# A fused attention and mixing kernel: the third batch's strided products later, their copies spread inside them, and the last sums tile by tile

## Chip, cores and metric

The kernel runs on one core of a Trainium2 chip. The metric is the device time of one execution in microseconds (us). Before the change it is 918.03 us, the median of three runs (916.94 to 919.47).

## Reference

Eight batches of 576 rows go through attention with eight heads of 64. Heads 0 to 3 see a local window of 32 rows, heads 4 to 7 see the earlier rows that lie a multiple of 32 away. The result `x` (576 x 512 per batch) goes through a mixer along the rows and a two-layer network.

```python
rel = pos[:, None] - pos[None, :]
mask_local = (rel >= 0) & (rel < stride)
mask_strided = (rel >= 0) & (pos[None, :] % stride == pos[:, None] % stride)
masks = np.stack([mask_local if h < H // 2 else mask_strided for h in range(H)], axis=0)
scores = np.where(masks[None, :, :, :], scores, -1000000000.0)
...
attn = attn / (np.sum(attn, axis=-1, keepdims=True) + 1e-09)
return np.matmul(attn, v).astype(np.float32)

xt = x.transpose(0, 2, 1)
h = xt @ U @ V
u = x + h.transpose(0, 2, 1)
ch = np.maximum(u @ w_ch1, 0.0) @ w_ch2
return (u + ch).astype(np.float32)
```

`U` is 576 x 32, `V` is 32 x 576, `w_ch1` is 512 x 2048 and `w_ch2` 2048 x 512.

## The kernel before

**Stages.** The network runs over nine stages n = 0 to 8. Stages 0 to 7 hold the first 512 rows of a batch, stage 8 the last 64 rows of all eight batches together. A stage has 16 steps `fc`, one for each 128 columns of the hidden layer. A step has twelve matmuls of 128 x 512 into `ph` (`gemm1`, L668), the ReLU on ScalarE (`gh`, L673), a correction on VectorE (`gl`, L674), and twelve matmuls into four sums `acc` (`gemm2`, L686). The matmuls are in threes, because each factor is split in a high and a low part: `gh` and `gl` of the hidden layer, `uh` and `ul` of `u`, parts 0 and 1 of a weight. `gemm2` of a step comes one step late, behind `gemm1` of the next. At a stage's end `finish(n)` (L693) adds the four sums to `xg` on VectorE and issues the output.

**The next batch meanwhile.** While stage n runs, the attention of batch n + 1 is made. The local heads use TensorE (`px`). For batches 2 to 7 the strided heads are vector work with all 18 rows of a class in one partition (`strided_heads`). GpSimd multiplies queries and keys (`tmp<-st`, L467) and VectorE reduces to scores `s_st` (L445). After the softmax the values are loaded into the place of the keys (`st`). GpSimd multiplies weights and values (`tmp<-st,s_st`, L495), and VectorE reduces again, to `st<-tmp` (L445). Row i needs i + 1 products of 64 elements; from row 9 on they are cut into two halves of 32 columns. Five `tmp` buffers lie between the two engines. ScalarE then copies the rows into `xg` and the tail `xt` (L512, L516). The mixing step follows: `mix_t` (L536), `mix_u` (L558), `mix_tail` (L567), the transposes to `bt` on VectorE (L638), and 32 transfers `raw<-bt` on SyncE's queue (L96). From `raw` ScalarE and VectorE make `uh` (L659) and `ul` (L660), which the next stage's `gemm1` reads.

**Order.** Every engine and queue works in its own order of instructions. A scheduler in the compiler sets it from the order of the program and its own estimate of times. In the program, `advance(slot)` is called twice per step, with slots 32 per stage. It takes from the generators as many pieces of work as `A_EARLY`, `A_LATE` and `A_TAIL` (first slot, last slot, count) and `S0` and `S1` (first and last slot of the strided work) ask for. `strided_end` draws what is left of the strided work before the copies. A reduce of the strided work is held behind the latest `finish` that the program has emitted (`reduced`, with `marks["out"]`).

**Start.** Stage 0 also converts the weights, which arrive as 64-bit numbers (`cv`, L131 and L132; `w`, L206), beside the strided scores of the third batch, b = 2.

Of the kernel before, what the change touches and what calls it, by code (L numbers as in the profile page):

```python
# [16 lines left out]
ATT_BUFS = 5  # L17
NSP = 2
N_EARLY = 17
N_LATE = 47  # L20
N_STRIDED = 66
LAG = 1
CLA = 4
N_FIRST = 6
N_LEAD = 4
BEHIND = 5
A_EARLY = (5, 28, N_EARLY)
A_LATE = (2, 26, N_LATE)
A_TAIL = (4, 20, 8)
S0 = {2: 16, **{b: 32 * (b - 1) - 12 for b in range(3, 8)}}  # L30
S1 = (12, 12)
ORDER0 = (2, 3, 0, 1)
WARM = {0: 8, 1: 8}
PAIR = 2 * 576 + 18 * 65
# [3 lines left out]
def fused_kernel(ctx, tc, pairs, strided, U, V, w_in, masks, eye, out):  # L38
# [53 lines left out]
    def psx1():  # L92
        return psx2()[:, 0, :]
# [121 lines left out]
            next(wl["gen"])  # L215
            wl["n"] += 1

    xgs, tails, tsts, o_str = {}, {}, {}, {}
    halves = [slice(64 * hh, 64 * hh + 64) for hh in range(2)]

    def load_qk(b, pr):
# [225 lines left out]
    def strided_heads(b):  # L447

        st = wide_buffer("st")
        sq, sk = (st[:, x * NCH * D:(x + 1) * NCH * D].rearrange("p (i d) -> p i d", d=D) for x in range(2))  # L450
        if b == NSP:
            nc.gpsimd.tensor_copy(out=st[0:1, 0:1], in_=word_of[units.index((10, None))])
        dma(out=st, in_=strided[b - NSP, :, 0:2 * NCH * D])
        yield
        s_st = att([128, NCH, NCH], "s_st")
        nc.gpsimd.memset(s_st, 8.0 * NEG)
        late = []

        def flush(n):
            while len(late) > n:  # L460
                late.pop(0)()

        for i in range(NCH):
            for j0 in range(0, i + 1, 9):
                n = min(9, i + 1 - j0)
                tmp = att([128, 9, D], "tmp")
                nc.gpsimd.tensor_tensor(out=tmp[:, 0:n], in0=sk[:, j0:j0 + n], in1=sq[:, i:i + 1].broadcast_to([128, n, D]),  # L467
                                        op=ALU.mult)
                late.append(lambda tmp=tmp, n=n, i=i, j0=j0: reduced(
                    out=s_st[:, i, j0:j0 + n], in_=tmp[:, 0:n], axis=AX.X, op=ALU.add))  # L470
# [12 lines left out]
        nc.vector.tensor_reduce(out=m_st, in_=s_st, axis=AX.X, op=ALU.add)  # L483
        nc.vector.tensor_scalar(out=m_st, in0=m_st, scalar1=1e-9, scalar2=None, op0=ALU.add)
        nc.vector.reciprocal(out=m_st, in_=m_st)
        nc.vector.tensor_tensor(out=s_st, in0=s_st, in1=m_st.broadcast_to([128, NCH, NCH]), op=ALU.mult)
        yield
        o_st = sq
        o_str[b] = o_st
        for i in range(NCH):  # L490
            step = D if i < 9 else D // 2
            for d0 in range(0, D, step):
                tmp = att([128, (i + 1) * step], "tmp")
                tv = tmp.rearrange("p (j d) -> p j d", d=step)
                nc.gpsimd.tensor_tensor(out=tv, in0=sv[:, 0:i + 1, d0:d0 + step],  # L495
                                        in1=s_st[:, i, 0:i + 1].broadcast_to([128, i + 1, step]), op=ALU.mult)
                late.append(lambda tv=tv, i=i, d0=d0, step=step: reduced(
                    out=o_st[:, i, d0:d0 + step], in_=tv.rearrange("p j d -> p d j"), axis=AX.X, op=ALU.add))
                flush(1)
                yield  # L500
        flush(0)
        yield

    def strided_copies(b):
        xg, xt = x_tiles(b)
        tb = 64 * (b % 2)
        o_st = o_str[b]
        for h in range(4):
            rows = slice(32 * h, 32 * h + 32)
            cs = slice(256 + D * h, 256 + D * h + D)  # L510
            for i4 in range(4):
                nc.scalar.copy(out=xg[32 * i4:32 * i4 + 32, :, cs], in_=o_st[rows, i4:16:4, :])  # L512
                if i4 % 2:
                    yield
            for i4 in range(2):
                nc.scalar.copy(out=xt[tb + 32 * i4:tb + 32 * i4 + 32, cs], in_=o_st[rows, 16 + i4, :])  # L516
            yield

    ud = dp.tile([B // 2, 128, DM], F32, name="ud", bufs=1)

# [95 lines left out]
    def attention(b):  # L616
        if b >= NSP:
            yield from local_pairs(b)
            yield "strided"
            yield from strided_copies(b)  # L620
            yield from mix_t(b)
            yield
            yield from mix_u(b)
            yield from mix_tail(b)
            yield from transposes(b)
        else:
            yield from mix_tail(0)
# [47 lines left out]
        marks.setdefault("gl", []).append(low.ins)  # L675
        return gh, gl

    def gemm2(n, fc, gh, gl):
        if fc == 0:
            accs[n] = [ps_acc.tile([128, 2, 512], F32, name="acc") for _ in range(2)]  # L680
        for s in range(4):
            cs = slice(128 * s, 128 * s + 128)
            if fc == 0 and n == 0:
                nc.tensor.matmul(accs[n][s // 2][:, s % 2, :], Vst[:, cs], tsts[n], start=True, stop=False)
            for i, (gt, part) in enumerate(((gh, 0), (gh, 1), (gl, 0))):
                last = nc.tensor.matmul(accs[n][s // 2][:, s % 2, :], gt[:, cs], w_parts[fc, 1][:, part, :],  # L686
                                        start=(fc == 0 and i == 0 and n > 0), stop=(fc == NFC - 1 and i == 2))
        marks.setdefault("acc", []).append(last.ins)

    def finish(n):  # L690
        for s in range(4):
            ot = xgs[n][:, s, :]
            last = nc.vector.tensor_tensor(out=ot, in0=accs[n][s // 2][:, s % 2, :], in1=ot, op=ALU.add)  # L693
# [158 lines left out]
```

## Time and profile before

| | |
|---|---|
| median of three runs | 918.03 us |
| profiled execution | 918.08 us |
| its span | 916.0 us |
| granted TensorE clock, mean | 0.993 |
| ScalarE busy | 253.2 us (28%) |
| VectorE busy | 548.3 us (60%) |
| GpSimd busy | 339.4 us (37%) |

The profile was taken in one execution. A row of its timeline gives the start in us from the start of the span, the duration, the engine, the source line, the operation and `out<-in` with the shapes, and how many such instructions ran one after another. In brackets stands how long the engine was idle before the row, and what released it. `SPq` and `ACTq` are the DMA issues of SyncE and ScalarE. A row of the groups gives a line's count, busy time, mean duration in ns, and idle time before it. A row of the waits gives who waited for what, the total, the number, and the longest.

The chain that ended last runs through `acc` and `ph`:

```profile
PE acc L686 40%; PE ph L668 39%; PE px L397 1%; DMA w<-in_w_dram 1%; PE px L357 1%; PE px L379 1%; DVE s_st L445 1%; PE px L536 1%; PE px L558 1%; DVE cv L132 1%; DMA st<-in_strided_dram 1%; DVE w L206 1%; DMA od<-x 1%; DVE gl L674 0%; POOL tmp L467 0%
```

### The profile page before, as it was taken

How to read it: one execution, taken by the hardware profiler on the slowest of the kernel's cores; microseconds unless marked ns; L12 is line 12 of the kernel's file. 1: busy time of each engine (PE TensorE's matmuls, PEld its weight loads, DVE VectorE, ACT ScalarE, POOL GpSimd, SP SyncE). 2: the span in 40 equal slices, each digit the busy share in tenths (PEclk: the TensorE clock that was granted, in tenths of full speed). 3: DMA queues.
4: the chain of work that ended last, by engine and by line, in shares of the span. 5: the costliest groups of instructions: out<-in, count | busy, mean ns of one | idle time of the engine just before them, and what ended most of it. 6: DMA issues, size and time to landing. Idle time of an engine off the chain costs nothing.

```text
span 916.0 us, 16587 instructions
## 1 busy us (share of the span) xinstructions
PE 893.4 (98%) x6862; PEld 714.1 (78%) x6862; DVE 548.3 (60%) x899; ACT 253.2 (28%) x501; POOL 339.4 (37%) x378
## 2 busy tenths in 40 slices
PE   7899989999999999999999999999999999999997
PEld 4677768887888787878887888878787888888885
DVE  4678997856786588738873877477754331122111
ACT  3456422241224122521242123312241211121110
POOL 1232484636563475429450946175620000000000
PEclk9899999999999999999999999999999999999999
DMA  9869313210331015011401050103200230001001
GB/s 355 308 211 357 118 44 116 72 53 3 86 135 42 12 52 183 1 53 31 165 28 53 21 187 28 53 9 124 91 1 3 57 116 23 1 1 47 0 1 47
DMA packets 30843, 75.27 MB, mean 82 GB/s; under 512 B 6464, under 2 KB 14672, under 8 KB 28848
## 3 DMA queue, kind: packets, MB, share of 16 engines
q1 hardware_dynamic: 29360, 71.07, 22.6%
q0 software_dynamic: 1088, 2.62, 0.9%
q8 instruction: 54, 0.88, 0.4%
q10 hardware_dynamic: 320, 0.52, 0.2%
q14 instruction: 21, 0.17, 0.1%
HBM read 54.14 MB, written 11.67 MB: 72 GB/s over the span
## 4 chain that ended last, share of the span: by engine, by line
PE 84%; DVE 4%; DMA 2%; POOL 1%; issue 1%; ACT 1%; SPq 0%; DVEq 0%; POOLq 0%; ACTq 0%
PE acc L686 40%; PE ph L668 39%; PE px L397 1%; DMA w<-in_w_dram 1%; PE px L357 1%; PE px L379 1%; DVE s_st L445 1%; PE px L536 1%; PE px L558 1%; DVE cv L132 1%; DMA st<-in_strided_dram 1%; DVE w L206 1%; DMA od<-x 1%; DVE gl L674 0%; POOL tmp L467 0%
## 5 line engine op out<-in xcount | busy, mean ns | idle before, releaser
L674 DVE SCALAR_TENSOR_TENSOR gl<-ph,gh 128x512 fp32r<-128x512 f32 x144 | 98.5, 685 | 233.7 <-ACT gh L673 232.9
L467 POOL TENSOR_TENSOR tmp<-st 128x576 f32<-128x576 f32 (+6 forms) x162 | 177.0, 1128 | 127.6 <-DMA st<-in_strided_dram 71.7
L668 PE MATMUL ph<-uh,w 128*128 128x512 f32 x648 | 215.4, 391 | 0.0
L673 ACT ACTIVATE gh<-ph 128x512 fp32r<-128x512 f32 x144 | 85.7, 597 | 449.0 <-PE ph L668 424.8
L686 PE MATMUL acc<-w,gh 128*128 128x512 f32 x648 | 196.3, 391 | 0.0
L495 POOL TENSOR_TENSOR tmp<-st,s_st 128x448 f32<-128x448 f32 (+7 forms) x162 | 137.0, 876 | 128.2 <-DVE st L445 51.2
L686 PEld LDWEIGHTS acc<-w,gh 128*128 128x128 f32 x648 | 121.2, 188 | 26.8 <-issue 1.2
L668 PEld LDWEIGHTS ph<-uh,w 128*128 128x128 f32 x648 | 121.7, 188 | 26.0
L445 DVE TENSOR_REDUCE st<-tmp 128x64 f32<-128x64 f32 (+8 forms) x162 | 135.6, 882 | 2.6 <-POOL tmp L495 2.1
L668 PE MATMUL ph<-ul,w 128*128 128x512 f32 x324 | 126.4, 390 | 0.0
L686 PE MATMUL acc<-w,gl 128*128 128x512 f32 x324 | 121.8, 391 | 4.2 <-DVE gl L674 4.2
L445 DVE TENSOR_REDUCE s_st<-tmp 128x9 f32<-128x576 f32 (+6 forms) x162 | 86.4, 561 | 14.0 <-POOL tmp L467 13.4
L686 PEld LDWEIGHTS acc<-w,gl 128*128 128x128 f32 x324 | 60.8, 188 | 18.7 <-DVE gl L674 5.9
L668 PEld LDWEIGHTS ph<-ul,w 128*128 128x128 f32 x324 | 60.8, 188 | 12.5
L512 ACT COPY xg<-st 32x256 f32<-32x256 f32 x96 | 38.8, 404 | 10.7 <-DVE st L445 9.0
L660 DVE TENSOR_TENSOR ul<-raw,uh 128x256 fp32r<-128x256 f32 x64 | 25.4, 432 | 12.9 <-ACT uh L659 12.5
L693 DVE TENSOR_TENSOR xg<-acc,xg 128x512 f32<-128x512 f32 x36 | 22.7, 682 | 17.4 <-PE acc L686 17.4
L659 ACT CAST uh<-raw 128x256 fp32r<-128x256 f32 x64 | 23.2, 404 | 19.5 <-DMA raw<-bt 10.2
L668 PE MATMUL ph<-uh,w0a 128*128 128x512 f32 x72 | 24.1, 391 | 0.0
L668 PE MATMUL ph<-uh,w1a 128*128 128x512 f32 x72 | 23.9, 391 | 0.0
L668 PE MATMUL ph<-uh,w2a 128*128 128x512 f32 x72 | 23.9, 391 | 0.0
L668 PE MATMUL ph<-uh,w6a 128*128 128x512 f32 x72 | 23.8, 392 | 0.0
(266 smaller groups left out, 1231.6 us busy)
## 6 DMA issues: line engine op xcount, KB each, us to landing
w<-in_w_dram SPq DMA_DIRECT2D x9, 1024.0 KB, 13.3
raw<-bt SPq DMA_DIRECT2D x256, 32.0 KB, 1.8
out_dram<-xg SPq DMA_DIRECT2D x32, 256.0 KB, 5.2
v<-in_pairs_dram SPq DMA_DIRECT2D x12, 585.0 KB, 5.1
st<-in_strided_dram SPq DMA_DIRECT2D x6, 1152.0 KB, 5.5
qk<-in_pairs_dram SPq DMA_DIRECT2D x12, 576.0 KB, 6.1
late<-in_pairs_dram SPq DMA_DIRECT2D x8, 585.0 KB, 8.2
late<-in_pairs_dram SPq DMA_DIRECT2D x8, 576.0 KB, 8.1
```

Of the source, the lines that this page charges most:

```text
L132: nc.vector.scalar_tensor_tensor(out=i, in0=lo_w, scalar=29, in1=i, op0=ALU.logical_shift_right, op1=ALU.bitwise_or)
L445: nc.vector.tensor_reduce(**what)
L467: nc.gpsimd.tensor_tensor(out=tmp[:, 0:n], in0=sk[:, j0:j0 + n], in1=sq[:, i:i + 1].broadcast_to([128, n, D]), op=ALU.mult)
L495: nc.gpsimd.tensor_tensor(out=tv, in0=sv[:, 0:i + 1, d0:d0 + step], in1=s_st[:, i, 0:i + 1].broadcast_to([128, i + 1, step]), op=ALU.mult)
L512: nc.scalar.copy(out=xg[32 * i4:32 * i4 + 32, :, cs], in_=o_st[rows, i4:16:4, :])
L659: nc.scalar.copy(out=hi, in_=raw[:, t, :, :, dc, :])
L660: nc.vector.tensor_tensor(out=lo, in0=raw[:, t, :, :, dc, :], in1=hi.bitcast(F32), op=ALU.subtract)
L668: last = nc.tensor.matmul(ph, w_parts[fc, 0][:, part, 128 * dc:128 * dc + 128], ut[:, dc, :], start=(dc == dcs[0] and i == 0), stop=(dc == ...
L673: marks.setdefault("gh", []).append(nc.scalar.activation(out=gh, in_=ph, func=AF.Relu).ins)
L674: low = nc.vector.scalar_tensor_tensor(out=gl, in0=ph, scalar=0.0, in1=gh.bitcast(F32), op0=ALU.max, op1=ALU.subtract)
L686: last = nc.tensor.matmul(accs[n][s // 2][:, s % 2, :], gt[:, cs], w_parts[fc, 1][:, part, :], start=(fc == 0 and i == 0 and n > 0), stop= ...
L693: last = nc.vector.tensor_tensor(out=ot, in0=accs[n][s // 2][:, s % 2, :], in1=ot, op=ALU.add)
```

## The change

Four things change. The third batch's strided work begins at slot 20 instead of 16 and ends eight slots later. The strided products start with rows 16 and 17 and then take rows 0, 4, 8, 12, then 1, 5, 9, 13 and so on; `strided_copies` is gone, and each group's copies stand inside the generator, one group behind. The counts of `advance` are set in two parts, one up to the strided work and one behind it. In stage 8 the fourth sum lies in the bank of `px`, and the last step's `gemm2` runs tile by tile, each held behind the one before.

```diff
-N_LATE = 47
-N_STRIDED = 66
+N_LOCAL = 20
+N_REST = 16
+N_STRIDED = 74
...
-A_LATE = (2, 26, N_LATE)
+A_LATE = (3, 12, 26)
+A_SECOND = (1, 19, 27)
...
-S0 = {2: 16, **{b: 32 * (b - 1) - 12 for b in range(3, 8)}}
-S1 = (12, 12)
+S0 = {2: 20, **{b: 32 * (b - 1) - 12 for b in range(3, 8)}}
+S1 = (20, 12)
...
-        for i in range(NCH):
-            step = D if i < 9 else D // 2
...
-            for i4 in range(4):
-                nc.scalar.copy(out=xg[32 * i4:32 * i4 + 32, :, cs], in_=o_st[rows, i4:16:4, :])
-                if i4 % 2:
+        done = []
+        for i4 in (4, 0, 1, 2, 3, None):
+            for i in () if i4 is None else range(16, NCH) if i4 == 4 else range(i4, 16, 4):
+                step = D if i < 9 else D // 2
...
+            flush(0)
+            done.append(i4)
+            if len(done) == 1:
+                continue
+            i4 = done[-2]
...
+            for h in range(4):
+                rows = slice(32 * h, 32 * h + 32)
+                cs = slice(256 + D * h, 256 + D * h + D)
+                if i4 < 4:
+                    nc.scalar.copy(out=xg[32 * i4:32 * i4 + 32, :, cs], in_=o_st[rows, i4:16:4, :])
+                else:
+                    for x in range(2):
+                        nc.scalar.copy(out=xt[tb + 32 * x:tb + 32 * x + 32, cs], in_=o_st[rows, 16 + x, :])
+                if h % 2:
                     yield
...
             yield "strided"
-            yield from strided_copies(b)
...
+            pair = [ps_acc.tile([128, 2, 512], F32, name="acc") for _ in range(2)]
+            accs[n] = [pair[s // 2][:, s % 2, :] for s in range(4)]
+            if n == B:
+                accs[n][3] = psx1()
...
-    while pend:
-        gemm2(*pend.pop(0))
+    gemm2(*pend[0])
+    for s in range(4):
+        with tc.issue_after(marks["acc"][-1]):
+            gemm2(*pend[1], (s,))
     finish(NB - 1)
```

What this moves is shown at three places on VectorE. The line numbers of after are two to six higher than those of before.

In stage 0, from the third late `gl` on, before (`cv` and `w` are the conversion of weights, `s_st<-tmp` the third batch's reduces):

```order
L674 SCALAR_TENSOR_TENSOR gl<-ph,gh 128x512
L445 TENSOR_REDUCE s_st<-tmp 128x9
L638 STREAM_TRANSPOSE bt<-xg 128x4x4x32 x2
L445 TENSOR_REDUCE s_st<-tmp 128x4
L131 TENSOR_SCALAR cv<-cv 128x1024
L206 TENSOR_TENSOR w_1572<-cv,w_1572 128x2x512
L445 TENSOR_REDUCE s_st<-tmp 128x9
L674 SCALAR_TENSOR_TENSOR gl<-ph,gh 128x512
```

and after:

```order
L677 SCALAR_TENSOR_TENSOR gl<-ph,gh 128x512
L641 STREAM_TRANSPOSE bt<-xg 128x4x4x32 x2
L133 TENSOR_SCALAR cv<-cv 128x1024
L208 TENSOR_TENSOR w_1572<-cv,w_1572 128x2x512
L677 SCALAR_TENSOR_TENSOR gl<-ph,gh 128x512
```

Three reduces are gone from between the two `gl`; they and nine others now stand behind `finish(0)`.

At the end of stage 1, before (`xg<-acc,xg` is `finish(1)`, `st<-tmp` the reduces of the next batch's second products, whose widths stand in the row as 64 or 32 columns):

```order
L674 SCALAR_TENSOR_TENSOR gl<-ph,gh 128x512
L660 TENSOR_TENSOR ul<-raw,uh 128x4x2x32 x5
L693 TENSOR_TENSOR xg<-acc,xg 128x512 x4
L445 TENSOR_REDUCE st<-tmp 128x64 x7
L674 SCALAR_TENSOR_TENSOR gl<-ph,gh 128x512
```

and after:

```order
L677 SCALAR_TENSOR_TENSOR gl<-ph,gh 128x512
L663 TENSOR_TENSOR ul<-raw,uh 128x4x2x32
L485 TENSOR_REDUCE m_st<-s_st 128x18
L486 TENSOR_SCALAR m_st<-m_st 128x18
L487 RECIPROCAL m_st<-m_st 128x18
L488 TENSOR_TENSOR s_st<-s_st,m_st 128x324
L699 TENSOR_TENSOR xg<-acc,xg 128x512 x4
L663 TENSOR_TENSOR ul<-raw,uh 128x4x2x32 x4
L447 TENSOR_REDUCE st<-tmp 128x32 x3
L677 SCALAR_TENSOR_TENSOR gl<-ph,gh 128x512
```

The four additions of `finish(1)` now stand ahead of the last four `ul`, and part of the softmax has moved behind the `gl`.

At the end of stage 3, before:

```order
L660 TENSOR_TENSOR ul<-raw,uh 128x4x2x32 x5
L693 TENSOR_TENSOR xg<-acc,xg 128x512 x4
L445 TENSOR_REDUCE st<-tmp 128x64 x7
L674 SCALAR_TENSOR_TENSOR gl<-ph,gh 128x512
L445 TENSOR_REDUCE st<-tmp 128x64
L674 SCALAR_TENSOR_TENSOR gl<-ph,gh 128x512
```

and after:

```order
L663 TENSOR_TENSOR ul<-raw,uh 128x4x2x32 x5
L699 TENSOR_TENSOR xg<-acc,xg 128x512 x4
L447 TENSOR_REDUCE st<-tmp 128x32 x4
L447 TENSOR_REDUCE st<-tmp 128x64 x2
L677 SCALAR_TENSOR_TENSOR gl<-ph,gh 128x512
L447 TENSOR_REDUCE st<-tmp 128x64
L677 SCALAR_TENSOR_TENSOR gl<-ph,gh 128x512
```

The seven reduces of rows 0 to 6 that stood ahead of the first `gl` of the next stage are now four halves of rows 16 and 17 and the reduces of rows 0 and 4.

More of the change, by code (lines that the diff above doesn't have):

```diff
@@ L216, in load_ahead @@
             wl["n"] += 1
-    xgs, tails, tsts, o_str = {}, {}, {}, {}
+    xgs, tails, tsts = {}, {}, {}
     halves = [slice(64 * hh, 64 * hh + 64) for hh in range(2)]
@@ L488, in strided_heads @@
         o_st = sq
-        o_str[b] = o_st
-        for i in range(NCH):
-            step = D if i < 9 else D // 2
[L492 to L505, printed above, removed]
-        tb = 64 * (b % 2)
[L507 to L510, printed above, removed]
-            for i4 in range(4):
-                nc.scalar.copy(out=xg[32 * i4:32 * i4 + 32, :, cs], in_=o_st[rows, i4:16:4, :])
-                if i4 % 2:
-                    yield
-            for i4 in range(2):
-                nc.scalar.copy(out=xt[tb + 32 * i4:tb + 32 * i4 + 32, cs], in_=o_st[rows, 16 + i4, :])
-            yield
+        tb = 64 * (b % 2)
@@ new lines, in strided_heads @@
+        done = []
+        for i4 in (4, 0, 1, 2, 3, None):
+            for i in () if i4 is None else range(16, NCH) if i4 == 4 else range(i4, 16, 4):
+                step = D if i < 9 else D // 2
+                for d0 in range(0, D, step):
+                    tmp = att([128, (i + 1) * step], "tmp")
+                    tv = tmp.rearrange("p (j d) -> p j d", d=step)
+                    nc.gpsimd.tensor_tensor(out=tv, in0=sv[:, 0:i + 1, d0:d0 + step],
+                                            in1=s_st[:, i, 0:i + 1].broadcast_to([128, i + 1, step]), op=ALU.mult)
+                    late.append(lambda tv=tv, i=i, d0=d0, step=step: reduced(
+                        out=o_st[:, i, d0:d0 + step], in_=tv.rearrange("p j d -> p d j"), axis=AX.X, op=ALU.add))
+                    flush(1)
+                    yield
+            flush(0)
[3 more added lines that the diff above has]
+            i4 = done[-2]
+            assert len(marks["out"]) == b - 1
+            xg, xt = x_tiles(b)
+            for h in range(4):
[7 more added lines that the diff above has]
+                if h % 2:
+                    yield
@@ L676, in gemm1, with gemm2 @@
         return gh, gl
-    def gemm2(n, fc, gh, gl):
+    def gemm2(n, fc, gh, gl, tiles=range(4)):
         if fc == 0:
-            accs[n] = [ps_acc.tile([128, 2, 512], F32, name="acc") for _ in range(2)]
-        for s in range(4):
+            pair = [ps_acc.tile([128, 2, 512], F32, name="acc") for _ in range(2)]
+            accs[n] = [pair[s // 2][:, s % 2, :] for s in range(4)]
+            if n == B:
+                accs[n][3] = psx1()
+        for s in tiles:
             cs = slice(128 * s, 128 * s + 128)
             if fc == 0 and n == 0:
-                nc.tensor.matmul(accs[n][s // 2][:, s % 2, :], Vst[:, cs], tsts[n], start=True, stop=False)
+                nc.tensor.matmul(accs[n][s], Vst[:, cs], tsts[n], start=True, stop=False)
             for i, (gt, part) in enumerate(((gh, 0), (gh, 1), (gl, 0))):
-                last = nc.tensor.matmul(accs[n][s // 2][:, s % 2, :], gt[:, cs], w_parts[fc, 1][:, part, :],
+                last = nc.tensor.matmul(accs[n][s], gt[:, cs], w_parts[fc, 1][:, part, :],
                                         start=(fc == 0 and i == 0 and n > 0), stop=(fc == NFC - 1 and i == 2))
@@ L692, in finish @@
             ot = xgs[n][:, s, :]
-            last = nc.vector.tensor_tensor(out=ot, in0=accs[n][s // 2][:, s % 2, :], in1=ot, op=ALU.add)
+            last = nc.vector.tensor_tensor(out=ot, in0=accs[n][s], in1=ot, op=ALU.add)
             if n == B:
@@ L744, in advance @@
         if gen is not None:
-            a0, a1, total = A_EARLY if n == 0 else A_LATE if n + 1 < B else A_TAIL
-            want = 10 ** 6 if k >= a1 else total * (k + 1 - a0) // (a1 - a0)
+            if 0 < n < B - 1:
+                a0, ak, a1 = A_SECOND if n == 1 else A_LATE
+                want = N_LOCAL * (k + 1 - a0) // (ak - a0) if k < ak else N_LOCAL + N_REST * (k + 1 - ak) // (a1 - ak)
+            else:
+                a0, a1, total = A_EARLY if n == 0 else A_TAIL
+                want = total * (k + 1 - a0) // (a1 - a0)
+            if k >= a1:
+                want = 10 ** 6
             while done < want:
@@ L767, in fused_kernel @@
             convert(2 * upto[min(NFC - 1, fc + CLA)])
-        if len(pend) > 1:
+        if len(pend) > 1 and step < len(steps) - 1:
             gemm2(*pend.pop(0))
```

## The prediction

> **What bounds the kernel now.** The page's busy times come first, then the table of waits on TensorE.
>
> ```profile
> PE 893.4 (98%) x6862; PEld 714.1 (78%) x6862; DVE 548.3 (60%) x899; ACT 253.2 (28%) x501; POOL 339.4 (37%) x378
> PE acc L686 <- DVE gl L674: 4.2, 4, 1.6
> PE acc L686 <- ACT gh L673: 0.6, 2, 0.3
> ```
>
> TensorE works through 98% of the 916.0 us span, and the change removes none of its matmuls. So the change is worth what it does to TensorE's waits, and to the stretch behind the last matmul. After the start there are few waits: four on `gl` (4.2 us) and two on `gh` (0.6 us). That limits the gain, not the loss: any input of a matmul that comes later than it does today adds its delay in full. I therefore ask, at each place where the engines' orders differ, when TensorE needs the input and when it would now have it.
>
> **Part 1, conversion stage, n = 0.** All four `gl` waits lie here, where VectorE converts weights, reduces the third batch's first products and makes `gl`. The order of VectorE is the same in both kernels up to the third of these `gl`, so the first three waits stay. Behind it, twelve reduces of `s_st` move beyond `finish(0)`. Three stood ahead of the fourth `gl`.
>
> ```profile
> 128.96 0.74 DVE L445 TENSOR_REDUCE s_st<-tmp 128x9 f32<-128x576 f32 x1
> ...
> 130.84 0.38 DVE L445 TENSOR_REDUCE s_st<-tmp 128x4 f32<-128x256 f32 x1
> ...
> 134.19 0.74 DVE L445 TENSOR_REDUCE s_st<-tmp 128x9 f32<-128x576 f32 x1
> 134.86 0.68 DVE L674 SCALAR_TENSOR_TENSOR gl<-ph,gh 128x512 fp32r<-128x512 f32 x1
> 135.59 0.50 PE L686 MATMUL acc<-w,gl 128*128 128x512 f32 x1 [0.74 <-DVE gl L674]
> ```
>
> By the starts of the rows behind them (129.62, 131.13 and 134.86) they hold VectorE 0.66, 0.29 and 0.67 us, 1.62 together. That `gl` then ends near 133.9, and TensorE asks for it at 135.59 - 0.74 = 134.85: the whole wait goes, **-0.74**. The removed reduces come back behind `finish(0)`:
>
> ```profile
> 160.39 1.28 DVE L693 TENSOR_TENSOR xg<-acc,xg 128x512 f32<-128x512 f32 x2
> 168.97 0.39 PE L686 MATMUL acc<-w1b,gl 128*128 128x512 f32 x1
> ```
>
> The next `gl` stands behind four of them, 2.1 us by rows like those above, so it ends near 164.5 and is wanted at 168.97; I cost their return at nothing. Should GpSimd be slow to make the four, 4 us are in hand.
>
> **Part 2, boundary from n = 1 to n = 2.** The third batch's products, four slots later and behind those reduces, end later, its copies too, and the load of the next batch's `st` waits for them. In TensorE's order the first product of the mixing step (L558) moves 17 matmuls back, into the next weight step.
>
> ```profile
> 223.40 0.63 PE L558 MATMUL px<-tst,Vst 96*128 96x512 f32 x2
> 227.45 20.14 SPq L96 DMA_DIRECT2D raw<-bt  x32
> 249.17 1.33 ACT L659 CAST uh<-raw 128x256 fp32r<-128x256 f32 x4 [0.62 <-DMA raw<-bt]
> 249.61 1.43 DVE L660 TENSOR_TENSOR ul<-raw,uh 128x256 fp32r<-128x256 f32 x4 [0.30 <-ACT uh L659]
> 252.13 2.48 DVE L693 TENSOR_TENSOR xg<-acc,xg 128x512 f32<-128x512 f32 x4 [1.09 <-PE acc L686]
> 252.84 0.39 PE L668 MATMUL ph<-uh,w0a 128*128 128x512 f32 x1
> 253.29 0.39 PE L668 MATMUL ph<-ul,w0a 128*128 128x512 f32 x1
> ```
>
> 17 matmuls at about 0.23 us are 3.9; less the 0.74 of part 1, the product starts 3.16 later on the clock, near 226.56. The 32 `raw` transfers are bound by their issue (20.14 / 32 = 0.63 us each) and follow the mixing step through the transposes, so they start near 230.6 instead of 227.45. `uh` for the second half follows 21.7 us after their start, at 252.3, and is ready near 252.8. TensorE, 0.74 earlier, wants it at 252.10: a wait of **0.7**. In before this `uh` was there 3.3 us ahead (249.58 against 252.84). (One matmul follows another after 0.227 us: two of them lie between 252.84 and 253.29.)
>
> Then the order of VectorE adds another: `xg` of `finish(1)`, four additions, now stand ahead of the four `ul`, where before `ul` came first. They start at 252.13 - 0.74 = 251.4, end at 253.85, and the first `ul` (about 0.36 us) is ready near 254.25. The third matmul, wanted at 253.3 after the first wait, is held for another **1.0**. With the step's last `w0a` matmul now near the end of its pair, `gh` costs the 0.3 that it costs at two other boundaries (table of waits above). Sum: **+2.0**. Bounds: the `ul` behind `xg` sets the sum. If the `raw` transfers shift by 2 us, the first wait is gone and this one grows by as much; only beyond a shift of about 4 us does each further microsecond cost its own length.
>
> **Part 3, boundaries 2 to 3, 3 to 4, 4 to 5, 5 to 6.** A batch's second products now begin with rows 16 and 17, each cut in two halves of 544 or 576 elements; before they began with 64, 128, 192 and so on. Seven short reduces stood ahead of the first `gl` of the new stage; now six stand there, four of them the longest there are.
>
> ```profile
> 445.72 1.69 POOL L495 TENSOR_TENSOR tmp<-st,s_st 128x64 f32<-128x64 f32 x4 [10.83 <-DMA st<-in_strided_dram]
> 445.26 2.48 DVE L693 TENSOR_TENSOR xg<-acc,xg 128x512 f32<-128x512 f32 x4 [0.65 <-PE acc L686]
> 447.66 3.71 DVE L445 TENSOR_REDUCE st<-tmp 128x64 f32<-128x64 f32 x7
> 451.29 0.68 DVE L674 SCALAR_TENSOR_TENSOR gl<-ph,gh 128x512 fp32r<-128x512 f32 x1
> 452.33 0.39 PE L686 MATMUL acc<-w0b,gl 128*128 128x512 f32 x1
> ...
> L445 DVE TENSOR_REDUCE st<-tmp 128x32 f32<-128x544 f32 x12 | 13.4, 1165 | 0.1
> L445 DVE TENSOR_REDUCE st<-tmp 128x32 f32<-128x576 f32 x12 | 14.6, 1219 | 0.0
> L495 POOL TENSOR_TENSOR tmp<-st,s_st 128x544 f32<-128x544 f32 x12 | 13.0, 1106 | 0.0
> ```
>
> From one start to the next a row is about 0.08 shorter than its duration (the `gl` of 0.68 is followed 0.6 later). So the four halves take 2 x 1.08 + 2 x 1.13 = 4.42 us. The other two, of 64 and 320 elements, stood among the seven, which took 3.63 us (447.66 to 451.29) for 1792 elements; 384 of these are 0.78. The six take 5.2. At 3 to 4 the `gl` would then end near 453.5. TensorE wants it at 452.33: about **+1.15**. The slack of today, 452.33 - 451.97 = 0.36, is used up first. GpSimd isn't the limit: from 445.72 its four halves take about 4.5 us and are ahead of the reduces throughout.
>
> ```profile
> 548.09 1.29 DVE L674 SCALAR_TENSOR_TENSOR gl<-ph,gh 128x512 fp32r<-128x512 f32 x2
> 549.14 0.39 PE L686 MATMUL acc<-w0b,gl 128*128 128x512 f32 x1
> 638.82 1.69 POOL L495 TENSOR_TENSOR tmp<-st,s_st 128x64 f32<-128x64 f32 x4 [10.83 <-DMA st<-in_strided_dram]
> 638.36 2.48 DVE L693 TENSOR_TENSOR xg<-acc,xg 128x512 f32<-128x512 f32 x4 [0.65 <-PE acc L686]
> 644.39 0.68 DVE L674 SCALAR_TENSOR_TENSOR gl<-ph,gh 128x512 fp32r<-128x512 f32 x1
> 645.43 0.39 PE L686 MATMUL acc<-w0b,gl 128*128 128x512 f32 x1
> ```
>
> At 4 to 5 the first `gl` ends near 548.75 and has 0.39 in hand: again **+1.15**. At 5 to 6 the slack is 0.36, and the first of the halves now stands between the two pairs of `xg`, at 639.6, while its product ends at 638.82 + 1.11 = 639.93: VectorE waits 0.3 for it, **+1.45**.
>
> ```profile
> 347.38 1.09 DVE L660 TENSOR_TENSOR ul<-raw,uh 128x256 fp32r<-128x256 f32 x3 [1.82 <-ACT uh L659]
> 348.39 1.28 DVE L693 TENSOR_TENSOR xg<-acc,xg 128x512 f32<-128x512 f32 x2
> 355.18 1.28 DVE L674 SCALAR_TENSOR_TENSOR gl<-ph,gh 128x512 fp32r<-128x512 f32 x2
> 349.54 0.39 PE L668 MATMUL ph<-ul,w0a 128*128 128x512 f32 x1
> 356.01 0.40 PE L686 MATMUL acc<-w0b,gl 128*128 128x512 f32 x1
> ```
>
> At 2 to 3 two of the `xg` pass ahead of the three `ul`. They still start at 348.39, released by TensorE, so the first `ul` is ready near 350.05 instead of 347.8; the third matmul, due at 349.54, waits 0.4 to 0.5. The three `ul` that VectorE did before 348.39 now follow, so `xg` and `ul` are through near 352.15 (1.2 + 1.1 + 1.2 + 0.3 us from 348.39). The five reduces ahead of this `gl` take 4.42 and 0.13. The `gl` is ready near 357.35 and wanted at 356.01 + 0.4: 0.95 more. Sum **+1.4**.
>
> Bounds for part 3: with the durations of these rows, 0.8 to 1.6 at each place; the second `gl` stands one long reduce behind the first, but TensorE wants it only after the other eight matmuls of that group and twelve of `ph`, 4.5 us later.
>
> **A rule on the shared port.** Elsewhere in this trace six `ul` beside products of GpSimd took 0.53 us each, where the four at 249.61 took 0.36:
>
> ```profile
> 149.73 3.21 DVE L660 TENSOR_TENSOR ul<-raw,uh 128x256 fp32r<-128x256 f32 x6 [0.46 <-ACT uh L659]
> 150.26 2.39 POOL L495 TENSOR_TENSOR tmp<-st,s_st 128x64 f32<-128x64 f32 x4 [5.32 <-DVE ul L660]
> ```
>
> The Trainium skill ("SBUF — State Buffer", section "SBUF: two separate sides") says that VectorE and GpSimd share a port pair as an exclusive lock, so that a VectorE operation with two SBUF inputs waits for a whole GpSimd instruction that reads SBUF. By it, one of the `ul` at 2 to 3 would wait for a product of 1.1 us instead of a short one, 0.8 more there, and the time would be 924.9. The rows above bear it out in kind; I leave it out of the sum, since the order in which the two engines start there is open.
>
> **Part 4, copies and tail.** The copies of strided rows spread over ScalarE, which is busy 28% of the span; no matmul waits for them but through part 2: nothing more. At the end the fourth sum lies in another bank and the last twelve matmuls run tile by tile.
>
> ```profile
> 908.68 2.48 DVE L693 TENSOR_TENSOR xg<-acc,xg 128x512 f32<-128x512 f32 x4 [3.21 <-PE acc L686]
> 909.40 2.45 SPq L96 DMA_DIRECT2D out_dram<-xg  x4
> ```
>
> The first addition was released by the eighth of these matmuls, and now is by the sixth, 2 x 0.227 earlier. The outputs follow the first addition at once and are bound by their issue, so the end comes **0.45** earlier. Bounds: nothing, and the 0.9 by which the fourth sum's own matmuls could be hidden.
>
> **Sum.** -0.74 + 2.0 + 1.4 + 1.15 + 1.15 + 1.45 - 0.45 = **+5.96**. The profiled execution took 918.08 us, 2.08 outside its span, beside a median of 918.03 (916.94 to 919.47): **924.0 us**, 0.65% slower. A difference of 0.3%, 2.75 us, is about what a measurement of this kernel can tell from no change.
>
> **Rivals.**
> - *Not slower: VectorE isn't late at the boundaries.* The place is the first `gl` of each stage; the price is part 3, 5.15 us, and part 2. It decides if the six reduces take under 3.63 + 0.36 = 4.0 us, a fifth less than the rows say, and if the additions at 1 to 2 start early enough for the `ul` behind them. Then only the two gains are left: 918.08 - 0.74 - 0.45 = 916.9. For it speaks that every reduce had products beside it when measured, and GpSimd's come in another rhythm now; against it, that the same shapes differ by little wherever they stand. Chance 0.10.
> - *Only one side of this:* the reduces fit, but part 2 comes as worked out: 918.9. Chance 0.14.
> - *Faster: the conversion stage is relieved altogether.* If all four waits went, 4.24, with the tail and without parts 2 and 3: 913.4. The order says that three of them stay. Chance 0.07.
> - *Worse: part 2 grows.* Between the third batch's additions and transposes stands a reduce whose product GpSimd makes only near 228.3. Where that makes the `raw` transfers 6 us late instead of 3.16, TensorE waits 2 us more: 926.0. The late load of `st` speaks for it; against it, that the reduces there are short. Chance 0.09.
> - Forecast as summed, 921.5 to 926: chance 0.60.
>
> The range takes in the second rival and the worse one, and leaves out the first and the faster one (0.17) and a little of the worse: 918.3 to 926.5. Slower by over 0.3% holds the forecast and the worse rival, 0.69; within 0.3% lie the first two, 0.24; faster 0.07.
>
> **What would show it.** In the profile of after, the waits of `acc` on `gl` should number seven, three in the conversion stage and four at the boundaries with about 1 us each; `ph` should wait for `uh` and `ul` near 252 to 254 us and for `ul` near 350. The last additions should start two matmuls earlier against the last matmul. If the first `gl` of a stage follows six reduces and no matmul waits, part 3 is wrong; if the 32 `raw` transfers start before 229, the first wait of part 2 is.

## Result and the profile after

The changed kernel takes 925.62 us (median of four runs, 923.59 to 927.54) against 917.49 us before (916.15 to 919.47): ratio 1.0089, 95% interval 1.0063 to 1.0114. It is slower by about 0.9%, where 0.65% was forecast. Run twice more, beside before on the same chip, it gave ratios of 1.0086 (1.0062 to 1.0110) and 1.0073 (1.0056 to 1.0090). The profiled execution took 927.54 us with a span of 925.8 us.

From the page, and then the table of waits on TensorE (who waited for whom, us in total, number, longest):

```profile
PE 895.0 (97%) x6861; PEld 713.1 (77%) x6862; DVE 546.5 (59%) x899; ACT 253.0 (27%) x501; POOL 335.8 (36%) x378
PE acc L399 <- issue: 5.5, 3, 3.7
PE acc L692 <- DVE gl L677: 5.0, 5, 1.6
...
PE acc L692 <- ACT gh L676: 2.2, 2, 1.5
...
PE ph L671 <- DVE ul L663: 1.1, 2, 0.8
...
PE ph L671 <- ACT uh L662: 0.5, 1, 0.5
```

TensorE's busy time is much the same (895.0 against 893.4 us); the waits are others. In before the four waits on `gl` were all in stage 0. Of the five now, two are left there, and three stand at boundaries between stages:

```profile
124.46 0.50 PE L692 MATMUL acc<-w,gl 128*128 128x512 f32 x1 [1.03 <-DVE gl L677]
131.79 0.50 PE L692 MATMUL acc<-w,gl 128*128 128x512 f32 x1 [1.55 <-DVE gl L677]
255.14 0.50 PE L671 MATMUL ph<-uh,w0a 128*128 128x512 f32 x1 [0.49 <-ACT uh L662]
256.65 0.50 PE L671 MATMUL ph<-ul,w0a 128*128 128x512 f32 x1 [0.77 <-DVE ul L663]
262.65 1.20 PE L692 MATMUL acc<-w0b,gh 128*128 128x512 f32 x4 [0.72 <-ACT gh L676]
354.55 0.50 PE L671 MATMUL ph<-ul,w0a 128*128 128x512 f32 x1 [0.35 <-DVE ul L663]
361.31 1.20 PE L692 MATMUL acc<-w0b,gh 128*128 128x512 f32 x4 [1.49 <-ACT gh L676]
460.30 0.50 PE L692 MATMUL acc<-w0b,gl 128*128 128x512 f32 x1 [0.76 <-DVE gl L677]
557.93 0.50 PE L692 MATMUL acc<-w0b,gl 128*128 128x512 f32 x1 [0.88 <-DVE gl L677]
655.56 0.50 PE L692 MATMUL acc<-w0b,gl 128*128 128x512 f32 x1 [0.76 <-DVE gl L677]
```

Read down the rows and the five boundaries appear in turn: three waits at 1 to 2 (255 to 263 us), two at 2 to 3 (354 to 361), and one on `gl` at each of the next three.

A ledger shows what these waits cost. In each stage I take the start of the first matmul with `w2a`, which stands just behind the boundary, in both profiles. For stage 0 and stage 3 the rows are, of before and then of after:

```profile
60.80 0.40 PE L668 MATMUL ph<-uh,w2a 128*128 128x512 f32 x1
...
357.86 0.39 PE L668 MATMUL ph<-uh,w2a 128*128 128x512 f32 x1
```

```profile
64.32 0.40 PE L671 MATMUL ph<-uh,w2a 128*128 128x512 f32 x1
...
364.59 0.40 PE L671 MATMUL ph<-uh,w2a 128*128 128x512 f32 x1
```

The difference is 3.52 us in stage 0 and 6.73 in stage 3. Taking each difference from the next gives the stretch between two of these matmuls; the two last columns are the same kernel's other profiles (e8 and e10 below).

| stretch | forecast | first profile | second | third |
|---|---|---|---|---|
| start, up to `w2a` of stage 0 | 0 | +3.52 | -0.11 | +2.66 |
| stage 0 | -0.74 | -1.87 | -1.79 | -1.36 |
| boundary 1 to 2 | +2.0 | +2.85 | +2.78 | +3.14 |
| boundary 2 to 3 | +1.4 | +2.23 | +1.52 | +1.49 |
| boundary 3 to 4 | +1.15 | +1.39 | +1.34 | +1.36 |
| boundary 4 to 5 | +1.15 | +0.79 | +0.79 | +0.77 |
| boundary 5 to 6 | +1.45 | +1.36 | +1.36 | +1.38 |
| last matmul to the end of the span | -0.45 | -0.48 | -0.59 | -0.56 |
| all, from `w2a` of stage 0 | +5.96 | +6.28 | +5.41 | +6.24 |

A profile's total is the span's end less the start of `w2a` in stage 0, against 855.2 us before; the stretches behind `w2a` of stage 6, which are left out, cancel to 0.01. Spans are read to 0.1 us, so the last two rows hold to about 0.1. The start is no part of the change: no engine's order differs there, and it came out 0.1 us early once, and 2.7 and 3.5 us late.

### The profile page after: what moved, and what is told of

Same layout as the page of the kernel before. It is cut to its first block, busy times and chain, and to the rows that moved or that the text cites. A ratio compares the mean times of both kernels' runs of the same rounds, so it can differ in the third digit from the quotient of the medians.

```text
span 925.8 us, 16580 instructions
## 1 busy us (share of the span) xinstructions
PE 895.0 (97%) x6861; PEld 713.1 (77%) x6862; DVE 546.5 (59%) x899; ACT 253.0 (27%) x501; POOL 335.8 (36%) x378
## 4 chain that ended last, share of the span: by engine, by line
PE 81%; DVE 7%; DMA 1%; SPq 1%; issue 1%; POOL 1%; ACT 0%; DVEq 0%; POOLq 0%; ACTq 0%
PE acc L692 38%; PE ph L671 37%; DVE st L447 2%; PE px L399 1%; DVE xg L699 1%; PE px L692 1%; PE px L359 1%; DMA st<-in_strided_dram 1%; SPq L98 1%; PE px L381 1%; DVE cv L134 1%; PE px L540 1%; DVE s_st L447 1%; PE px L562 1%; DVE gl L677 1%
## 5 line engine op out<-in xcount | busy, mean ns | idle before, releaser
L469 POOL TENSOR_TENSOR tmp<-st 128x576 f32<-128x576 f32 (+6 forms) x162 | 174.4, 1119 | 158.2 <-DMA st<-in_strided_dram 81.1
L692 PE MATMUL acc<-w,gh 128*128 128x512 f32 x630 | 190.3, 390 | 0.0
L499 POOL TENSOR_TENSOR tmp<-st,s_st 128x576 f32<-128x576 f32 (+7 forms) x162 | 137.3, 873 | 100.9 <-DMA st<-in_strided_dram 56.1
L692 PEld LDWEIGHTS acc<-w,gh 128*128 128x128 f32 x630 | 118.3, 188 | 25.2 <-issue 0.2
L447 DVE TENSOR_REDUCE st<-tmp 128x32 f32<-128x544 f32 (+8 forms) x162 | 134.3, 878 | 5.0 <-POOL tmp L499 5.0
L692 PE MATMUL acc<-w,gl 128*128 128x512 f32 x315 | 118.3, 391 | 2.6 <-DVE gl L677 2.6
L550 DVE TENSOR_TENSOR ta<-px,ta 32x512 f32<-32x512 f32 x21 | 14.4, 687 | 26.1 <-ACT ta L548 25.6
```

The costliest lines, as they stand in the source:

```text
L447: nc.vector.tensor_reduce(**what)
L550: nc.vector.tensor_tensor(out=ta, in0=ps_a[32 * j:32 * j + 32, :], in1=ta, op=ALU.add)
L692: last = nc.tensor.matmul(accs[n][s], gt[:, cs], w_parts[fc, 1][:, part, :], start=(fc == 0 and i == 0 and n > 0), stop=(fc == NFC - 1 and ...
```

## Experiments

Each is compared with before by runs on the same chip, and by the same ledger. "Counted from `w2a`" means from the first `w2a` of stage 0 to the end of the span.

### e1: the order of rows alone, in the kernel before

```diff
-        for i in range(NCH):
+        for i in (16, 17, *(i for i4 in range(4) for i in range(i4, 16, 4))):
```

> The kernel before with one edit: the strided products start with rows 16 and 17, then take every fourth row; the copies stay at the end, the third batch and the tail stay as they were. Counted from the first matmul of w2a in stage 0 to the end of the span (855.2 us before, 861.5 us after). Theory (long reduces ahead of a gl): four halves and a short reduce, 4.55 us, stand where 3.63 us stood, with a slack of 0.36, so about 0.55 us at each of five boundaries, 857.7 us, and waits of acc on gl at the boundaries. Rival (the copies inside the products make the waits, or their order costs nothing): 855.2 us and no such wait.

Ratio 1.0035 (1.0020 to 1.0051). The ledger gives 858.4 us (forecast 857.7, rival 855.2), 3.2 more than before: 0.70, 1.19, 0.72, 0.67 and 0.75 us at the five boundaries, and 0.83 less in stage 0. So about half of the loss at the boundaries needs nothing but the order of rows. The timeline of VectorE and TensorE at 1 to 2:

```profile
253.23 4.61 DVE L445 TENSOR_REDUCE st<-tmp 128x32 f32<-128x544 f32 x5
257.75 0.69 DVE L674 SCALAR_TENSOR_TENSOR gl<-ph,gh 128x512 fp32r<-128x512 f32 x1
258.49 0.50 PE L686 MATMUL acc<-w0b,gl 128*128 128x512 f32 x1
```

Five reduces take 4.6 us, the `gl` behind them ends at 258.44, and TensorE uses it 0.05 us later.

### e2: additions behind `ul`, in the changed kernel

```diff
+                marks["ul"] = nc.vector.tensor_tensor(out=lo, in0=raw[:, t, :, :, dc, :], in1=hi.bitcast(F32), op=ALU.subtract).ins
...
+            with tc.issue_after(marks["ul"]) if n < B else nullcontext():
+                last = nc.vector.tensor_tensor(out=ot, in0=accs[n][s], in1=ot, op=ALU.add)
```

> The changed kernel with one edit: the additions of finish are held behind the last ul of the next stage. Counted as before (861.5 us for the changed kernel). Theory (additions ahead of ul cost TensorE at the boundaries 1 to 2 and 2 to 3): the waits of ph on ul, 0.77 and 0.35 us, go, and at 2 to 3 the reduces and with them gh and gl come about 2 us earlier, so that of 2.85 and 2.23 us at these two boundaries 1.9 and 0.3 are left: 858.6 us. Rival (the reduces alone set the time there): 861.5 us.

Ratio 1.0054 (1.0035 to 1.0074); 860.0 us counted from `w2a`, between the two. At 1 to 2 it leaves 2.12 us of 2.85, at 2 to 3 1.41 of 2.23 (1.5 in the changed kernel's other two profiles, so little is gained there), and no matmul waits for `ul`. At 2 to 3 the reduces still set the time, as the rival had it: the wait now bears the name of `gh` (1.29 us), and the `gl` follows right behind. In the first profile of the changed kernel it is the same:

```profile
359.76 1.01 ACT L519 COPY xt<-st 32x64 f32<-32x64 f32 x4 [6.58 <-DVE st L447]
360.68 1.06 ACT L676 ACTIVATE gh<-ph 128x512 fp32r<-128x512 f32 x2
357.52 4.46 DVE L447 TENSOR_REDUCE st<-tmp 128x32 f32<-128x544 f32 x5
361.90 0.67 DVE L677 SCALAR_TENSOR_TENSOR gl<-ph,gh 128x512 fp32r<-128x512 f32 x1
362.63 0.50 PE L692 MATMUL acc<-w0b,gl 128*128 128x512 f32 x1
```

On ScalarE four copies of row 16 stand ahead of `gh`, and wait for the second reduce. But TensorE uses `gl` at 362.63, 0.06 us after it is made: with an earlier `gh` it would have waited for `gl` instead.

### e3: the first `gl` ahead of the reduces, in the changed kernel

The strided products begin eight pieces of work later (`N_STRIDED` grows by eight for it), and their reduces are held behind the latest `gl` (`held` is set for them); the products and their order are the same.

```diff
+        for _ in range(8):
+            yield
         o_st = sq
...
+            with tc.issue_after(marks["gl"][-1]) if held else nullcontext():
+                nc.vector.tensor_reduce(**what)
```

> The changed kernel with the same products in the same order, but their reduces held behind the latest gl that the program has made, and the products begun eight pieces of work later, so that the first gl of each new stage stands ahead of all of them. Theory (reduces ahead of gl make the waits at the last four boundaries): 2.2, 1.4, 0.8 and 1.4 us there shrink to 0.3 in all, so 861.5 becomes 856.2 us, with the third batch's late mixing step still paid at 1 to 2. Rival (the order of rows or the spread copies cost in themselves): 861 us.

Ratio 1.0030 (1.0013 to 1.0048); 857.1 us counted from `w2a`. The last four boundaries cost 0.21, 0.05, 0.34 and 0.04 us, 0.64 in all, where they cost 5.77 in the first profile and 5.0 in the others. 1 to 2 still costs 2.41, and 0.33 comes back inside stage 6. The 0.9 us above the forecast is what stage 0 gains less here: 1.00 instead of 1.87. VectorE and TensorE at 3 to 4:

```profile
446.97 2.48 DVE L702 TENSOR_TENSOR xg<-acc,xg 128x512 f32<-128x512 f32 x4 [0.25 <-PE acc L695]
452.88 0.69 DVE L680 SCALAR_TENSOR_TENSOR gl<-ph,gh 128x512 fp32r<-128x512 f32 x1 [3.42 <-ACT gh L679]
453.48 4.48 DVE L448 TENSOR_REDUCE st<-tmp 128x32 f32<-128x544 f32 x4
454.03 0.39 PE L695 MATMUL acc<-w0b,gl 128*128 128x512 f32 x1
```

VectorE now idles 3.42 us and waits for `gh`, and that costs nothing: the same reduces run behind the `gl`. This shows the mechanism of part 3, with rows and copies in the order of the change. The products start later here too, which this run alone doesn't separate; e1 has the long reduces ahead of `gl` with the products at their old time, and there the waits come.

### e4 and e9: the tail alone, in the kernel before

```diff
+            if n == B:
+                accs[n][3] = psx1()
...
+    for s in range(4):
+        with tc.issue_after(marks["acc"][-1]):
+            gemm2(*pend[1], (s,))
```

> The kernel before with the tail of the change alone: fourth sum in the bank of px and the last matmuls tile by tile. From the start of the last matmul to the end of the span: 6.84 us before, 6.36 after. Theory: 6.4 us, and nothing else changes (853 us from w2a of stage 0 to the last matmul's start less 4.7, that is 848.4 as before). Rival (the gain of the tail comes from elsewhere): 6.84 us.

> The kernel before with the tail of the change alone, once more, since its first ratio (0.997) was larger than the 0.3 to 0.5 us that its profile shows in the tail. Theory (the tail is all that it gains; the rest was the start, which differs between executions): 6.3 to 6.5 us from the last matmul to the end, and a ratio between 0.998 and 1.000. Rival (the tail's code gains 3 us): ratio 0.997 again.

From the last matmul's start to the end 6.50 and 6.29 us instead of 6.84, the gain of part 4. The ratios are 0.9969 (0.9952 to 0.9985) and 0.9992 (0.9976 to 1.0009): the first was more than the tail can give, and the second agrees with it. Counted from `w2a`, 855.3 and 853.8 us; what differs from 855.2 beyond the tail is stage 0 (+0.48 and -0.75, with an order equal to before's). There the first wait on `gl` was 1.33 us in e4 and missing in e9, where before has 0.91. So the ledger of e4 shows no gain behind the start. The start does: it took 59.08 us, the least of all profiles, at a mean granted clock of 1.00 against 0.92 in before. The seven runs of e4 had mean clocks of 0.995 to 0.998, the 22 of before beside them 0.993 in the median. The tail alone is the best of the versions tried, though its gain of 0.3 to 0.5 us is less than the ratios can tell.

### e5: copies behind `gh`, in the changed kernel

The copies of rows 16 and 17 come last, each held behind the latest `gh`.

```diff
+            if i4 == 4:
+                continue
...
+                with tc.issue_after(marks["gh"][-1]):
+                    nc.scalar.copy(out=xt[tb + 32 * x:tb + 32 * x + 32, 256 + D * h:256 + D * h + D],
+                                   in_=o_st[32 * h:32 * h + 32, 16 + x, :])
```

> The changed kernel with one edit: the copies of rows 16 and 17 come last and are held behind the latest gh, so that no copy stands ahead of the first gh of a stage on ScalarE; the scheduler also puts ul ahead of the additions at 2 to 3 then, and five reduces instead of six ahead of gl. Counted from the first w2a of stage 0 to the end (861.5 us for the changed kernel). Theory (reduces ahead of gl are the wait; copies ahead of gh only show it under another name): the waits on gh fall to about 0.3 us each, but acc waits for gl at all five boundaries, 0.7 us each at the last four as in the kernel with the order alone: 859.5 us. Rival (the copies ahead of gh cost what the boundaries lose): hardly a wait at the last four boundaries, 857 us.

Ratio 1.0050 (1.0029 to 1.0072); 861.2 us counted from `w2a`. The last four boundaries cost 0.17, 0.73, 0.88 and 0.75 us, near the forecast of 0.7 but for the first, where `ul` and additions also changed places. The waits on `gh` are 0.3 us each, and `acc` waits for `gl` eight times. 1 to 2 grew to 3.73 us: five reduces instead of three stand ahead of its `gl`, and `ul` was waited for 1.38 us. The total missed both forecasts (859.5 and 857) by that and by stage 0, where the first `gl` was waited for 2.01 us. The theory holds for three boundaries. At 3 to 4 and 5 to 6, where five reduces instead of six stand ahead of `gl`, the cost is 0.73 and 0.75 us here and 0.72 and 0.75 in e1, with the copies in another place; so there the copies cost nothing of their own, and the sixth reduce makes the 0.6 us by which the changed kernel is worse.

### e6: the third batch later, in the kernel before

```diff
-S0 = {2: 16, **{b: 32 * (b - 1) - 12 for b in range(3, 8)}}
-S1 = (12, 12)
+S0 = {2: 20, **{b: 32 * (b - 1) - 12 for b in range(3, 8)}}
+S1 = (20, 12)
```

> The kernel before with one edit: the third batch's strided work four slots later and its end eight slots later. Counted as before (855.2 us before). Theory: the fourth gl wait of stage 0 goes (-0.7 to -1), and at 1 to 2 the raw transfers come late and the additions stand ahead of ul, +2.0 to +2.9, with nothing at the later boundaries: about 856.9 us. Rival (the late third batch costs nothing by itself): 854.4 us.

Both were wrong. The ratio is 1.0111 (1.0083 to 1.0138), with 864.2 us counted from `w2a`; stage 0 gains 1.93 us and 1 to 2 loses 10.99. The `raw` transfers start 10.5 us late against before, once the earlier shift of -0.40 us is taken off, and two `ul` stand ahead of the last `gl` of stage 1, beside GpSimd's products (SyncE, VectorE, GpSimd and TensorE):

```profile
237.54 20.16 SPq L96 DMA_DIRECT2D raw<-bt  x32
249.63 3.91 DVE L660 TENSOR_TENSOR ul<-raw,uh 128x256 fp32r<-128x256 f32 x2
253.47 0.67 DVE L445 TENSOR_REDUCE s_st<-tmp 128x8 f32<-128x512 f32 x1
238.34 14.59 POOL L467 TENSOR_TENSOR tmp<-st 128x576 f32<-128x576 f32 x12
254.40 0.68 DVE L674 SCALAR_TENSOR_TENSOR gl<-ph,gh 128x512 fp32r<-128x512 f32 x1
255.13 0.80 PE L686 MATMUL acc<-w,gl 128*128 128x512 f32 x1 [3.20 <-DVE gl L674]
```

The two `ul` take 3.91 us where four take 1.43 with GpSimd idle. The `gl` behind them holds TensorE 3.20 us, and then TensorE's granted clock falls to half:

```profile
255.00:259.00 4.00, 3.78 (x8) 2.48 (x8) 3.93 (x9) 0.48 (x1) 0.00 (x0) 0.50 0.24 55
259.00:263.00 4.00, 2.34 (x5) 1.43 (x6) 3.76 (x10) 1.32 (x4) 0.46 (x2) 0.50 0.91 283
...
264.00:265.00 1.00, 1.00 (x4) 0.77 (x4) 0.80 (x2) 0.00 (x0) 1.00 (x2) 0.64 1.08 428
265.00:266.00 1.00, 1.00 (x6) 0.83 (x5) 0.87 (x3) 0.00 (x0) 1.00 (x3) 1.00 1.06 368
```

(The columns are the stretch, its length, busy time and count of PE, PEld, DVE, ACT and POOL, the granted clock, the DMA share and GB/s.) Over nine microseconds a matmul takes twice its time. The rest of the loss is the waits for `uh` and `ul` that part 2 describes, 0.83 and 0.92 us here. In the changed kernel, which sets the counts of `advance` anew (`A_SECOND`), the transfers are 3.85 us late (part 2 below), and `gl` is not held up like this; whether these counts alone prevent it was not tested.

### e7: a version meant to keep the gains

Before with the tail of the change, `S0[2] = 20`, `S1 = (16, 12)`, and the additions of `finish` behind `ul` as in e2.

> The kernel before with the tail of the change, the third batch's strided work from slot 20 with its end four slots later instead of eight, and the additions of finish held behind ul; rows in their old order, copies at the end. Counted as before (855.2 us before). Theory: -0.7 to -1 in stage 0, nothing or up to 0.4 at the boundaries, -0.4 in the tail: 854 us, so about 1 us or 0.1% faster than before. Rival (a late third batch can't be had without the cost at 1 to 2): 856.5 us.

Ratio 0.9999 (0.9986 to 1.0012), no difference; 855.1 us counted from `w2a`. Stage 0 gains 1.79, the tail 0.63, and 1 to 2 loses 2.56: the `raw` transfers start at 232.78, 5.0 us late against before once the earlier shift of 0.38 us is taken off, and `uh` is waited for 1.06 us. Both totals missed, the forecast since 1 to 2 costs more, the rival since stage 0 gains more. The rival's reason holds: with the end four slots later instead of eight the transfers come no earlier (3.85 us late in the changed kernel, see part 2 below), and the late third batch is paid at 1 to 2.

### e8 and e10: the changed kernel again

> The changed kernel once more, to separate its start from the rest. Theory (the 3.5 us that its profile lost before w2a of stage 0 differ from execution to execution and are no part of the change): from w2a to the end 861.5 us again, and a start that lies within 2 us of before's 60.8. Rival (the changed program starts later): a start near 64.

> The changed kernel a third time. Its medians stand 7.7 to 8.1 us above before, its two profiles 5.4 and 6.3 us from w2a of stage 0 on. Theory (the rest lies in the start, which by chance was late in most executions): 860.5 to 861.5 us from w2a to the end again, with a start between 60 and 64 us. Rival (a stretch behind the start is sometimes longer, as where the additions, ul and the products meet at 2 to 3): more than 862 us from w2a to the end.

Their ledgers stand in the table: 860.6 and 861.4 us counted from `w2a`, starts at 60.69 and 63.46 us, near what the two theories had. The stretch that differs most behind the start is 2 to 3, 2.23 us once and 1.5 twice. The rows of VectorE and GpSimd there, of the first profile and then of the second:

```profile
356.28 1.32 DVE L663 TENSOR_TENSOR ul<-raw,uh 128x256 fp32r<-128x256 f32 x1
357.52 1.15 DVE L447 TENSOR_REDUCE st<-tmp 128x32 f32<-128x544 f32 x1
356.21 1.10 POOL L499 TENSOR_TENSOR tmp<-st,s_st 128x544 f32<-128x544 f32 x1
```

```profile
352.66 0.44 DVE L663 TENSOR_TENSOR ul<-raw,uh 128x256 fp32r<-128x256 f32 x1
353.02 1.16 DVE L447 TENSOR_REDUCE st<-tmp 128x32 f32<-128x544 f32 x1
352.78 1.29 POOL L499 TENSOR_TENSOR tmp<-st,s_st 128x544 f32<-128x544 f32 x1
```

The last `ul` takes 1.32 us in the one and 0.44 in the other, and the reduces behind it start that much later. In the first a product of GpSimd started 0.07 us ahead of this `ul`, in the second the `ul` was 0.12 us ahead of the product, and in the third 0.02 us. This is the difference.

What stays open: the medians of the three comparisons lie 7 to 8 us above before, the profiles of one execution 5.4 to 6.3 counted from `w2a`. The start differs by up to 3.6 us between profiles of one kernel, and can hold the rest. It goes in part with TensorE's granted clock. Behind `w2a` of stage 0 the mean clock was 1.00 up to 908 us in the profiles of before, of e4 and of the changed kernel's three; up to `w2a` it was 0.92 in before, 1.00 in e4, and 0.92, 0.92 and 0.89 in the changed kernel's. A late start is no mark of the changed program: e1, e4, e6, e7 and e9, which start as before, came between 59.08 and 62.97 us. Every run lists its mean clock. If all chips are taken together, the changed kernel's medians at 0.991, 0.993 and 0.995 lie 7.1, 6.6 and 6.9 us above before's at the same clock (6, 4 and 3 runs against 5, 16 and 12). So a part of the 7 to 8 us goes with a lower clock in the changed kernel's runs; about a microsecond beyond the ledger stays open, since only profiled executions show their start.

## Why the prediction held, point by point

**What bounds the kernel** was right: behind the start, everything is in TensorE's waits and behind its last matmul. The waits on `gl` were to number seven; they number five, six and seven in the three profiles, since the first of stage 0 is not always there and the one at 2 to 3 is partly named after `gh`.

**The sum** came out near the ledgers (+5.96 against +6.28, +5.41 and +6.24), but that is partly luck. The five boundaries cost 8.6, 7.8 and 8.1 us, where 7.15 was forecast, and stage 0 gave back 0.6 to 1.1 us more than forecast, most of which is not the change's doing (part 1).

**Part 1**, -0.74: the fourth wait on `gl` is gone in all three profiles. It is gone in all eight profiles of kernels with the later third batch, and it stands, at 0.74 to 0.77 us, in all four of the others (before, e1, e4, e9). Stage 0 shows -1.4 to -1.9, since the first of the other three waits varies: 0.91 us in the profile of before, none in the first two of after, 0.58 in the third. Kernels whose stage 0 was left as it was show -0.83, +0.48 and -0.75 in that stretch (e1, e4, e9), so no more than the fourth wait is put down to the change.

**Part 2**, +2.0: the transfers came as forecast.

```profile
232.95 20.15 SPq L98 DMA_DIRECT2D raw<-bt  x32
```

They start 5.50 us later than in before. TensorE is itself 1.65 later there (3.52 - 1.87), so they are 3.85 us late against it, which is 17 matmuls of 0.227 (forecast 3.9). In the second profile, with its earlier start, they begin at 229.40, also 3.85 late. The waits are the three forecast, 0.49 on `uh` (forecast 0.7), 0.77 on `ul` (1.0) and 0.72 on `gh` (0.3); that they add up to the forecast is luck, since two are smaller and one is larger. Each costs TensorE about 0.27 us more than its bracket says. The row before a wait counts as busy for 0.39 us, though the next matmul could start after 0.227; and the first matmul after one takes longer: in the timeline of after the matmul behind 460.30 starts at 460.64, 0.34 us later instead of 0.227. 1.98 + 3 x 0.27 is 2.8, as measured. This restart was missing in the sum.

**Part 3**, +5.15: right in its mechanism, which e3 shows by taking the reduces away from ahead of `gl`, and near in size: 5.77 and twice 5.0. Six reduces were put at 5.2 us. VectorE at 3 to 4 in after:

```profile
454.40 5.24 DVE L447 TENSOR_REDUCE st<-tmp 128x32 f32<-128x544 f32 x6
459.55 0.69 DVE L677 SCALAR_TENSOR_TENSOR gl<-ph,gh 128x512 fp32r<-128x512 f32 x1
```

They take 5.15, far from the 4.0 at which they would have fitted. The term of 3 to 4 was too small (1.15 against 1.39) by about the restart, 0.11 us behind the wait, and the 0.06 from the end of `gl` to its use. The term of 4 to 5 was too large (0.79 against 1.15): it took the reduces to start as in before. The rows there, of before and then of after:

```profile
541.50 1.29 DVE L693 TENSOR_TENSOR xg<-acc,xg 128x512 f32<-128x512 f32 x2 [0.57 <-PE acc L686]
542.71 0.47 DVE L660 TENSOR_TENSOR ul<-raw,uh 128x256 fp32r<-128x256 f32 x1
544.30 3.70 DVE L445 TENSOR_REDUCE st<-tmp 128x64 f32<-128x64 f32 x7
```

```profile
549.64 2.48 DVE L699 TENSOR_TENSOR xg<-acc,xg 128x512 f32<-128x512 f32 x4 [1.16 <-PE acc L692]
552.04 5.24 DVE L447 TENSOR_REDUCE st<-tmp 128x32 f32<-128x544 f32 x6
```

From the first addition to the first reduce it takes 2.80 us in before and 2.40 in after, since a `ul` that stood between the additions now stands ahead of all four. At 5 to 6 the 0.3 us for which VectorE was to wait for its first product did not come, and the restart made up for it (1.36 against 1.45).

**The rule on the shared port** put 0.8 more at 2 to 3 (924.0 with it is 924.8, not 924.9). It came in one profile of three, as the 1.32 us of the last `ul`. The Trainium skill ("SBUF — State Buffer", section "SBUF: two separate sides") says that whichever starts first gets the pair for its whole instruction; the trace agrees, and so the cost is there in one execution and not in another.

**Part 4**: the tail gave 0.48 to 0.59, forecast 0.45. The first addition now starts 0.94 us ahead of the last matmul, in before 0.48 (908.68 against 909.16), so two matmuls earlier:

```profile
918.50 1.89 DVE L699 TENSOR_TENSOR xg<-acc,xg 128x512 f32<-128x512 f32 x3 [2.76 <-PE acc L692]
919.44 0.39 PE L692 MATMUL px<-w,gl 128*128 128x512 f32 x1
```

That the copies cost nothing was not quite right: at 1 to 2 the copies ahead of `gh` made its wait 0.72 instead of 0.3 (with the copies behind `gh`, in e5, it is 0.30). At 2 to 3 they only name a wait that `gl` would have had.

**The rivals**: the reduces did not fit; part 2 did not grow in the changed kernel, though e6 shows how it can. Of four waits in stage 0 only one went by the change.

## What to carry to other kernels

Where one engine is busy 97% of the time, an edit that moves work on the others is priced where their order changes: list what stands ahead of each input of the bound engine, and compare its sum with the slack there. A unit of work may move freely inside a stage and still cost at its edge, where a long instruction at the head of a queue stands ahead of a short one that is waited for. Moving the same reduces behind the short one takes the cost away, with no work saved.

## What the hardware showed that was not expected

A wait of 3.20 us on TensorE was followed by about nine microseconds at half the granted clock (e6), and one of 3.73 us in the start of the first profile of after by some three (0.64 and 0.50 of full speed from 58.2 to 62 us). Behind the start the granted clock stayed at 1.00 around waits of up to 2.01 us (e5). The Trainium skill ("TensorE: Matmul & The Clock Gate", section "Part 1: The HAM clock gate") has the clock fall after an idle window of about 3.4 us; the trace agrees in kind, and shows it at 3.20. But the length of one wait does not decide alone. In the start of before no wait near the fall is longer than 1.33 us (the one that ends at 27.64, behind one of 0.76 that ends at 25.64), and yet the clock fell:

```profile
30.00:34.00 4.00, 4.00 (x28) 3.06 (x34) 2.19 (x4) 0.74 (x1) 0.51 (x1) 0.50 0.65 205
```

TensorE had been busy there for only 0.67 of the two microseconds from 26 to 28. Where the clock falls, a wait is paid twice.

An operation of VectorE that reads two tiles in SBUF can take five times as long beside GpSimd's products: two `ul` took 3.91 us in e6, 1.95 each, against 0.36.

The start of one and the same kernel, up to `w2a` of stage 0, came between 60.7 and 64.3 us in three profiles, at a mean granted clock of 0.89 to 0.92. Differences of 0.3% between two kernels are therefore better read from a ledger behind the start than from two spans.
